# Top-k attention and capacity routing: a longer lag between the steps of a hand-ordered pipeline, and part of a division on VectorE

## The chip, the core and the metric

The kernel runs on one core of a Trainium2 chip. The core has five engines with instruction queues of their own, each working in order: TensorE (PE, with its weight loads shown as PEld), VectorE (DVE), ScalarE (ACT), GpSimd (POOL) and SyncE (SP, which here only issues transfers). They meet through semaphores: an instruction waits until others, on other engines, have finished. SBUF is the on-chip memory of 128 partitions, PSUM the memory that TensorE writes its results into. The metric is the device time of one execution, in microseconds.

## The reference

Attention over 8 batches, 8 heads, 576 positions and 64 dimensions, in which every row of scores keeps only its 32 largest; then a mixture of 8 experts in which each token goes to its best expert and each expert keeps at most 80 tokens.

```python
scores = scale * np.matmul(q, k.transpose(0, 1, 3, 2))
kth = np.partition(scores, -top_k, axis=-1)[..., -top_k:-top_k + 1]
mask = scores >= kth
scores = np.where(mask, scores, -1000000000.0)
scores = scores - np.max(scores, axis=-1, keepdims=True)
attn = np.exp(scores)
attn = attn / (np.sum(attn, axis=-1, keepdims=True) + 1e-09)
attn_out = np.matmul(attn, v)                     # (B, H, S, D)
x = attn_out.transpose(0, 2, 1, 3).reshape(B * S, H * D)
logits = x @ w_gate                               # 4608 tokens, 8 experts
expert_idx = np.argmax(logits, axis=1)            # gate_w: softmax weight of the best
# per expert e: the 80 tokens with the largest gate_w
out[tok_idx] = gate_w[tok_idx, None] * (np.maximum(x[tok_idx] @ w1[e], 0.0) @ w2[e])
```

## The kernel before

**Work.** `n` counts the 32 pairs of heads (8 batches times 4 pairs). Of each pair the 576 queries are cut into five tiles `t`: four of 128 rows, and one, `t = NF = 4`, that holds the last 64 rows of both heads. A unit is one head of one tile: 128 rows by 576 scores. So each `n` has 9 units (two each of the tiles 0 to 3, one of tile 4), and there are 288 units `i` and 160 tiles.

**Steps of one unit**, with the names used later (lines of the kernel before):

- `front` (L226, L233): PE makes the scores of a tile in the PSUM tile `sp`, of which there is one; ACT copies them scaled to SBUF, `s`.
- `parts` (L241): DVE takes the 8 largest of each of six blocks of a row, six MAX8 instructions into `cand`.
- `search`: from these 48, DVE takes three times the 8 largest (L252), knocking them out in between (L260). With the 24th largest as bias, ACT writes `sign`, whether each score is below it, with a count (L257). POOL multiplies scores and signs into `y` (L263, the product); DVE takes the 8 largest of `y`, that is, the next ones below (L265, the maximum), and picks the threshold by the count (L268, the pick, with an accumulator read behind it).
- `below` (L277, L279): the mask of scores under the threshold, on ACT for odd units and on POOL for even units.
- `turn_w` (L315 to L324), once per tile: PE transposes scores into the PSUM tiles `ab` (one buffer) and `cc` (two buffers) and adds the masks, scaled to be very negative; ACT takes the exponential into `wT`, first of `cc`, then of `ab`.
- `back` (L335): PE multiplies `wT` with v, into the free half of the same `cc`. v has a column of ones, so that the sums of the weights come out as well.
- `over` (L347): DVE takes the reciprocal of these sums, into `z_all`.
- `divide` (L358): the result times the reciprocal goes to `xn`, as two ACT instructions per tile.
- `norm` (L367 to L394), once per `n` in four pieces over later steps: SP stores `xn`; PE turns it (L201), ACT copies it (L375), PE multiplies it with the gate (L380), ACT copies the result (L387), and for three of four `n` DVE adds it to the logits (L391). Every second batch `gates` follows (L402 to L425), a dozen small DVE instructions.

**Order.** The order on each engine is the order in which `run` records it: it is written by hand, and no scheduler moves anything. `step(i)` records one step; the letters of a string say what comes when on DVE, with POOL and ACT instructions recorded where they fall:

```python
back = dict(a=0, b=1, c=1, d=1, e=1, y=2, g=3, h=4, m=4, H=3, M=3)
for c in "GybGcGdGeGGzag" if i % 2 else "GGbghHmMyGcGdGeGza":
```

`G` is one MAX8 of unit `i`; `a` to `e` are the three rounds and two knock-outs, `e` with the sign on ACT; `y` is the product, `g` the maximum, `h` and `H` the pick, `m` and `M` the mask, `z` the reciprocal. The number is the lag: `y=2` records in step `i` the product of unit `i - 2`. Even steps hold the masks and picks of two units, odd steps none. After the letters a step records `turn_w` for the tile whose last unit is `i - 4`, then `divide`, the `front` of unit `i + 4`, `back` for the tile of `i - 5`, at times the turn of the next q and k (`turn`, L201 and L214), and pieces of `norm`. Behind a half tile (`rest`), `back` of the tile before it comes first.

**Buffers.** `s` has 5 buffers (a tile each), `sign`, `y`, `wT` and `xn` 2, `mask` 3, `cand` 3, the other small tiles 4, v (`vb`) 3. q, k and v of `n + 2` are loaded by SP in the step of the unit (t = 2, h = 1) of `n`; in others SP also sends one transfer of expert weights or one that clears part of the output (`slow`).

After the loop come `route` (choosing tokens, mostly DVE) and the experts (mostly PE); neither is touched.

Of the kernel before, what the change touches and what calls it, by code (L numbers as in the profile page):

```python
# [27 lines left out]
def kernel(  # L28
# [11 lines left out]
    nc = tc.nc  # L40
# [108 lines left out]
    class Attention:  # L149


        def __init__(self, stack, lean):
            self.lean = lean
            pool = lambda name, bufs, **kw: stack.enter_context(tc.tile_pool(name=name, bufs=bufs, **kw))
            self.nat, self.qkp, self.rows = pool("nat", 1), pool("qkp", 2), pool("rows", 2)
            self.small, vpool = pool("small", 4), pool("vpool", 1)
            self.ps_s, self.ps_w, self.ps_c = (pool(n, k, space=PSUM) for n, k in (("ps_s", 1), ("ps_w", 1), ("ps_c", 2)))
            self.qk, self.turned, self.lg = {}, {}, {}
            self.s, self.top, self.cnt, self.y, self.mask, self.w, self.xn = ({} for _ in range(7))
            self.thr, self.z = thr_all, z_all  # L160
            self.odd = set()


            self.vb = []
            for j in range(1 if lean else 3):
                t = vpool.tile([P, NK, 2, D + 1], F32, name=f"vb{j}")
                nc.gpsimd.memset(t[:, :, :, D : D + 1], 1.0)
                nc.gpsimd.memset(t[: P - TL, NF, :, :], 0.0)
                self.vb.append(t)

            self.xT = vpool.tile([P, NK * P], F32, name="xT")
            nc.gpsimd.memset(self.xT[:, S:], 0.0)

        def load(self, n, b, hp):
            one = bass.ds(b, 1)
            tiles = []
            for name, src in (("qn", q), ("kn", k)):
                t = self.nat.tile([P, NK, 2, D], F32, name=name, tag=name)
                for h in range(2):
                    nc.sync.dma_start(  # L180
                        t[:, 0:NF, h, :],
                        src[one, 2 * hp + h, : NF * P, :].rearrange("o (c p) d -> p (o c) d", p=P))
                nc.sync.dma_start(
                    t[0:TL, NF, :, :], src[one, 2 * hp : 2 * hp + 2, NF * P :, :].rearrange("o h p d -> p (o h) d"))
                tiles.append(t)
            t = self.vb[n % len(self.vb)]
            for h in range(2):
                nc.sync.dma_start(
                    t[:, :NF, h, :D], v[one, 2 * hp + h, : NF * P, :].rearrange("o (c p) d -> p (o c) d", p=P))
            nc.sync.dma_start(  # L190
                t[P - TL :, NF, :, :D], v[one, 2 * hp : 2 * hp + 2, NF * P :, :].rearrange("o h p d -> p (o h) d"))
            self.qk[n] = tiles

        def four(self):
            return self.ps_s.tile([P, 4, 512], F32, name="sp", tag="sp")
# [20 lines left out]
        def front(self, n, t):  # L216

            qT, kT = self.turned[n]
            m = P if t < NF else TL
            i = n * UPP + 2 * t  # L220
            ps = self.four()
            for j in range(2):
                for h in range(2):
                    d = slice(D * h, D * h + D)
                    o = ps[:, 2 * h + j, :HS] if t < NF else ps[TL * h : TL * h + TL, j, :HS]
                    nc.tensor.matmul(o, lhsT=qT[d, t * P : t * P + m], rhs=kT[d, j * HS : (j + 1) * HS], start=True, stop=True)  # L226
            g = 2 if t < NF else 1
            s = self.rows.tile([P, 2 * S], F32, name="s", tag="s", bufs=2 if self.lean else 5)
            for h in range(g):
                self.s[i + h] = s[:, h * S : (h + 1) * S]  # L230
            for j in range(0, 2 * g, 2 if i == 0 else 2 * g):
                w = 2 if i == 0 else 2 * g
                nc.scalar.activation(s[:, j * HS : (j + w) * HS].rearrange("p (j c) -> p j c", c=HS), ps[:, j : j + w, :HS],  # L233
                                     Act.Copy, scale=TINY)
# [10 lines left out]
        def search(self, i):  # L245

            s, cand = self.s[i], self.top[i]
            top = self.top[i] = self.small.tile([P, G0 // 8 - 1, 8], F32, name="top", tag="top")
            w9 = self.small.tile([P, 16], F32, name="w9", tag="w9")
            for r in range(G0 // 8):  # L250
                dst = top[:, r, :] if r < G0 // 8 - 1 else w9[:, :8]
                nc.vector.max(out=dst, in_=cand)  # L252
                if r == G0 // 8 - 1:

                    sign = self.rows.tile([P, S], BF16, name="sign", tag="sign")
                    cnt = self.small.tile([P, 1], F32, name="cnt", tag="cnt")
                    nc.scalar.activation(sign, s, Act.Sign, bias=w9[:, 7:8], scale=-1.0, accum_out=cnt)  # L257
                yield
                if r < G0 // 8 - 1:
                    nc.vector.match_replace(out=cand, in_to_replace=dst, in_values=cand, imm_value=LOW)  # L260
                    yield
            y = self.rows.tile([P, S], F32, name="y", tag="y")
            nc.gpsimd.tensor_tensor(out=y, in0=s, in1=sign, op=Alu.mult)  # L263
            yield
            nc.vector.max(out=w9[:, 8:], in_=y)  # L265
            yield
            pick = self.small.tile([P, TOP_K - G0 + 1], F32, name="pick", tag="pick")
            nc.vector.scalar_tensor_tensor(out=pick, in0=past, scalar=cnt, in1=w9[:, 7:], accum_out=self.thr[:, i : i + 1],  # L268
                                           op0=Alu.is_equal, op1=Alu.mult)
            yield  # L270

        def below(self, i):

            self.top.pop(i)
            self.mask[i] = self.rows.tile([P, S], BF16, name="mask", tag="mask", bufs=3)
            if i in self.odd:
                nc.scalar.activation(self.mask[i], self.s[i], Act.Relu, bias=self.thr[:, i : i + 1], scale=-1.0)  # L277
                return
            nc.gpsimd.tensor_scalar(self.mask[i], self.s[i], self.thr[:, i : i + 1], None, op0=Alu.is_lt)  # L279
# [69 lines left out]
        def divide(self, n, t):  # L349
            if t == 0:  # L350
                self.xn[n] = self.rows.tile([P, NK, 2, D], F32, name="xn", tag="xn")
            cc = self.w.pop((n, t))
            for h in range(2):
                if t < NF:
                    p, o, j, m = slice(0, P), 2 * P + h * (D + 1), h, P
# [71 lines left out]
        def run(self, slow):  # L427

            units = []
            for n in range(NP):  # L430
                for t in range(NF):
                    units += [(n, t, 0), (n, t, 1)]
                units.append((n, NF, 2))
            self.odd = set(range(1, NU, 2))
            first, second = {}, {}
            later = []
            due = []
            drawn = []
            ready = {}

            def whole(i):
# [3 lines left out]
            def step(i, last):  # L445
                if 0 <= i < NU:
                    n, t, h = units[i]
                    if t == 2 and h == 1 and n + 2 < NP:
                        self.load(n + 2, *divmod(n + 2, HP))
                    if t in (1, 3) and h == 0 and slow and n:  # L450
                        slow.pop(0)()
                    if t == 0 and h == 0 and n + 1 < NP:
# [1 line left out]
                    first[i] = self.parts(i)  # L454


                back = dict(a=0, b=1, c=1, d=1, e=1, y=2, g=3, h=4, m=4, H=3, M=3)
                for c in "GybGcGdGeGGzag" if i % 2 else "GGbghHmMyGcGdGeGza":
                    if c == "G":
                        if 0 <= i < NU:  # L460
                            next(first[i])
# [3 lines left out]
                            second[i] = self.search(i)  # L465
                            next(second[i])
                    elif c == "z":
                        for u in drawn:
                            self.over(*u)
                    elif c in "mM":  # L470
                        if 0 <= i - back[c] < NU:
                            self.below(i - back[c])
                    elif i - back[c] in second:
                        next(second[i - back[c]])
                done = list(drawn)
                drawn.clear()

                def back():
                    if whole(i - 5):
                        self.back(*units[i - 5][:2])  # L480
                        drawn.append(units[i - 5][:2])


                rest = whole(i - 4) and units[i - 4][2] == 2
                if rest:
                    back()
                if whole(i - 4):
                    self.turn_w(*units[i - 4][:2])
                for u in done:
                    self.divide(*u)  # L490

                ends = [(n, range(NK) if n < NP - 1 else range(NF) if t < NF else range(NF, NK))
                        for n, t in done if t == NF or (n == NP - 1 and t == NF - 1)]
# [20 lines left out]
                    ready[later[-1]] = 0  # L514

            with tc.manual_schedule():
                self.load(0, 0, 0)
                self.load(1, *divmod(1, HP))
                nc.sync.dma_start(wg, moe_w_gate.rearrange("(c p) e -> p c e", p=P))
                self.turn(0)  # L520
                i = -4
                while i < NU + 6 or later:
                    step(i, i >= NU + 5)
                    i += 1
            assert not slow and not due

        def batch(self, b):

            for hp in range(HP):
                self.load(hp, b, hp)  # L530
                self.turn(hp)
                for t in range(NK):
                    self.front(hp, t)
# [381 lines left out]
```

## Time and profile before

| | |
|---|---|
| median of 3 runs | 994.47 us (993.04 to 995.51) |
| profiled execution: its own time | 994.13 us |
| its span, first to last instruction | 992.4 us |
| mean granted TensorE clock | 0.983 |
| attention loop | until about 868 us |
| POOL product L263 | 288, mean 1280 ns |
| POOL mask L279 | 144, mean 1722 ns |
| DVE maximum L265 | 288, mean 752 ns |
| ACT division L358 | 320, 86.6 us busy |

The span is what the profile shows of the execution. Busy time is the time in which an engine had an instruction running. Idle time before an instruction is put down to whoever released it last. Instructions on DVE and ACT overlap a little at their ends, so that the distance from start to start is shorter than a duration.

### The profile page before, as it was taken

To read this page: it belongs to the slowest core of one execution; us is meant where nothing else is said; L and a number is where in the kernel's file an instruction comes from. 1 tells how busy PE (TensorE), PEld (TensorE's weight loads), DVE (VectorE), ACT (ScalarE), POOL (GpSimd) and SP (SyncE) were. 2 spreads that over 40 slices of the span, in tenths; PEclk is the share of its full clock that TensorE was granted. 3 is DMA by queue.
4 is the path that set the end of the run, shared out by engine and by line. 5 is a ranking of instruction groups with operands and counts; after the bars stand their busy time and mean duration, and the time that the engine had idled before them with its cause. 6 is when DMAs were issued, how large, how long until landed. Compare 5 with 4: busy or idle time off the path is not lost.

```text
span 992.4 us, 35679 instructions
## 1 busy us (share of the span) xinstructions
PE 881.3 (89%) x13368; PEld 710.3 (72%) x13368; DVE 804.6 (81%) x4928; ACT 798.2 (80%) x1652; POOL 627.3 (63%) x474
## 2 busy tenths in 40 slices
PE   5899999999989999999899999999899998689996
PEld 3677777777767777777677777777677776578896
DVE  5798989898989898999989898989898989471110
ACT  3899999999989999999899999999899999501110
POOL 3677767676767777777677676766677777402111
PEclk9999999999999999999999999999999999979999
DMA  3445453333323233333111122222222200084921
GB/s 72 102 123 133 126 135 91 92 92 92 93 76 77 75 87 86 88 90 92 46 41 44 44 50 50 51 50 49 49 50 50 50 13 14 16 339 147 368 85 29
DMA packets 167797, 85.76 MB, mean 86 GB/s; under 512 B 117696, under 2 KB 154560, under 8 KB 167616
## 3 DMA queue, kind: packets, MB, share of 16 engines
q1 hardware_dynamic: 166592, 80.78, 29.1%
q0 software_dynamic: 1024, 2.62, 0.9%
q8 instruction: 107, 1.75, 0.7%
q14 instruction: 74, 0.61, 0.2%
HBM read 63.19 MB, written 20.19 MB: 84 GB/s over the span
## 4 chain that ended last, share of the span: by engine, by line
DVE 46%; PE 26%; ACT 15%; POOL 7%; issue 5%; DMA 1%; POOLq 0%; SPq 0%; DVEq 0%; ACTq 0%
DVE cand L241 15%; DVE w L265 11%; DVE cand L260 6%; PE cc L335 5%; DVE top L252 5%; ACT sign L257 5%; POOL y L263 5%; PE sp L226 4%; PE yp L799 4%; DVE pick L268 3%; ACT wT L324 3%; ACT mask L277 3%; PE sp L201 2%; DVE w L252 2%; POOL mask L279 2%
## 5 line engine op out<-in xcount | busy, mean ns | idle before, releaser
L241 DVE MAX8 cand<-s 128x8 f32<-128x96 f32 x1728 | 400.6, 246 | 9.0 <-ACT s L233 8.8
L263 POOL TENSOR_TENSOR y<-s,sign 128x576 f32<-128x576 f32 x288 | 365.3, 1280 | 65.9 <-ACT sign L257 65.9
L279 POOL TENSOR_SCALAR mask<-s,thr_all 128x576 bf16<-128x576 f32 x144 | 247.9, 1722 | 178.3 <-DVE pick L268 175.4
L335 PEld LDWEIGHTS cc<-vb,wT 128*64 128x64 f32 x5760 | 182.8, 139 | 113.6 <-ACT wT L324 100.1
L265 DVE MAX8 w<-y 128x8 f32<-128x576 f32 x288 | 216.4, 752 | 45.8 <-POOL y L263 45.8
L335 PE MATMUL cc<-vb,wT 128*64 128x65 f32 x5760 | 205.2, 226 | 42.7 <-ACT wT L324 42.7
L257 ACT ACTIVATE sign<-s,w 128x576 bf16<-128x576 f32 x288 | 225.2, 782 | 7.1 <-POOL y L263 3.0
L226 PE MATMUL sp<-both 64*128 64x288 f32 (+1 forms) x1280 | 203.2, 437 | 17.5 <-ACT part L387 9.5
L233 ACT ACTIVATE s<-sp 128x1152 f32<-128x1152 f32 (+1 forms) x161 | 167.4, 1040 | 12.2 <-PE sp L226 9.9
L315 PE MATMUL ab<-ident,s 128*128 128x128 f32 x1148 | 176.2, 283 | 0.0
L324 ACT ACTIVATE wT<-ab 128x1024 f32<-128x1024 f32 (+1 forms) x159 | 149.1, 937 | 0.0
L226 PEld LDWEIGHTS sp<-both 64*128 64x128 f32 (+1 forms) x1280 | 106.1, 180 | 56.4 <-ACT part L387 11.4
L315 PEld LDWEIGHTS ab<-ident,s 128*128 128x128 f32 x1148 | 127.9, 142 | 11.6 <-issue 0.9
L252 DVE MAX8 top<-cand 128x8 f32<-128x48 f32 x576 | 116.0, 201 | 4.5
L277 ACT ACTIVATE mask<-s,thr_all 128x576 bf16<-128x576 f32 x144 | 112.4, 781 | 6.9 <-DVE pick L268 6.5
L320 PEld LDWEIGHTS <-mask 128*128 128x128 bf16 x1440 | 94.2, 98 | 31.9 <-POOL mask L279 29.2
L260 DVE MATCH_REPLACE8 cand<-top,cand 128x48 f32<-128x48 f32 x576 | 110.9, 193 | 0.0
L358 ACT ACTIVATE xn<-cc,z_all 128x64 f32<-128x64 f32 (+1 forms) x320 | 86.6, 320 | 1.2 <-DVE z_all L347 0.8
L315 PE MATMUL cc<-ident,s 128*128 128x128 f32 x288 | 79.1, 275 | 0.0
L322 ACT ACTIVATE wT<-cc 128x256 f32<-128x256 f32 (+1 forms) x160 | 56.9, 356 | 16.8 <-PE cc L320 15.5
L268 DVE SCALAR_TENSOR_TENSOR pick<-past,cnt,w 128x9 f32<-128x9 f32 x288 | 60.3, 223 | 0.3 <-ACT xn L358 0.3
L257 ACT ACTIVATION_READ_ACCUMULATOR sign<-s,w 128x1 f32 x288 | 58.7, 204 | 0.0
(187 smaller groups left out, 909.4 us busy)
## 6 DMA issues: line engine op xcount, KB each, us to landing
w<-in_moe_w_dram SPq DMA_DIRECT2D x10, 2048.0 KB, 11.6
w<-in_moe_w_dram SPq DMA_DIRECT2D x24, 512.0 KB, 4.6
out_dram<-zero SPq DMA_DIRECT2D x9, 1024.0 KB, 6.5
qn<-in_q_dram SPq DMA_DIRECT2D x64, 128.0 KB, 2.5
kn<-in_k_dram SPq DMA_DIRECT2D x64, 128.0 KB, 2.5
vb<-in_v_dram SPq DMA_DIRECT2D x64, 128.0 KB, 2.7
xd<-xn SPq DMA_DIRECT2D x32, 256.0 KB, 3.8
qn<-in_q_dram SPq DMA_DIRECT2D x32, 32.0 KB, 2.3
```

The costliest lines, as they stand in the source:

```text
L226: nc.tensor.matmul(o, lhsT=qT[d, t * P : t * P + m], rhs=kT[d, j * HS : (j + 1) * HS], start=True, stop=True)
L233: nc.scalar.activation(s[:, j * HS : (j + w) * HS].rearrange("p (j c) -> p j c", c=HS), ps[:, j : j + w, :HS], Act.Copy, scale=TINY)
L241: nc.vector.max(out=cand[:, j, :], in_=s[:, j * S // NG : (j + 1) * S // NG])
L252: nc.vector.max(out=dst, in_=cand)
L257: nc.scalar.activation(sign, s, Act.Sign, bias=w9[:, 7:8], scale=-1.0, accum_out=cnt)
L260: nc.vector.match_replace(out=cand, in_to_replace=dst, in_values=cand, imm_value=LOW)
L263: nc.gpsimd.tensor_tensor(out=y, in0=s, in1=sign, op=Alu.mult)
L265: nc.vector.max(out=w9[:, 8:], in_=y)
L279: nc.gpsimd.tensor_scalar(self.mask[i], self.s[i], self.thr[:, i : i + 1], None, op0=Alu.is_lt)
L315: nc.tensor.matmul(dst[h][c], lhsT=sc[:, keys[c]], rhs=ident, start=c == 0 or (c == NF and h == 0), stop=False, is_transpose=True, skip_gr ...
L324: nc.scalar.activation(wT[:, : g * NF, :], ab.rearrange("p h c r -> p (h c) r")[:, : g * NF, :], Act.Exp, scale=scale / TINY)
L335: nc.tensor.matmul(cc[r : r + TL, o], lhsT=wT[:, h * NF + c if c < NF else 2 * NF + h, r : r + TL], rhs=vb[:, c, h if t < NF else r // TL, ...
```

## The change

- The lags grow: `y` 2 to 3, `g` 3 to 4, `h` and `m` 4 to 5, `H` and `M` 3 to 4; `turn_w` is recorded for unit `i - 6` (`LT`) and `back` for `i - 7`. Between `back` and the reciprocal lie two steps instead of one (`drawn`, three lists).
- A new letter `x` records `divide` two or three DVE instructions behind `z`, ahead of `turn_w`, where it stood behind `turn_w`. `z` moves forward in the string.
- For the tiles `t` = 0 and 1 the division is one DVE instruction, a product of the sums in PSUM with the reciprocals, over both heads. The others stay on ACT.
- Buffers: `s` 5 to 7, `sign` 2 to 3, `mask` 3 to 4, the small tiles 4 to 7.
- v's load is a function of its own, recorded two units later than q's and k's.

In the kernel after, the product is L266, the maximum L268, the pick L271, POOL's mask L282, `turn_w` L318 to L327, `back` L338, the reciprocal L350, the new DVE division L359, ACT's L367, the logit add L400.

```diff
--- before.py
+++ after.py
@@ -153,7 +153,7 @@
             self.lean = lean
             pool = lambda name, bufs, **kw: stack.enter_context(tc.tile_pool(name=name, bufs=bufs, **kw))
             self.nat, self.qkp, self.rows = pool("nat", 1), pool("qkp", 2), pool("rows", 2)
-            self.small, vpool = pool("small", 4), pool("vpool", 1)
+            self.small, vpool = pool("small", 7), pool("vpool", 1)
             self.ps_s, self.ps_w, self.ps_c = (pool(n, k, space=PSUM) for n, k in (("ps_s", 1), ("ps_w", 1), ("ps_c", 2)))
             self.qk, self.turned, self.lg = {}, {}, {}
             self.s, self.top, self.cnt, self.y, self.mask, self.w, self.xn = ({} for _ in range(7))
@@ -183,13 +183,16 @@
                 nc.sync.dma_start(
                     t[0:TL, NF, :, :], src[one, 2 * hp : 2 * hp + 2, NF * P :, :].rearrange("o h p d -> p (o h) d"))
                 tiles.append(t)
+            self.qk[n] = tiles
+
+        def load_v(self, n, b, hp):
+            one = bass.ds(b, 1)
             t = self.vb[n % len(self.vb)]
             for h in range(2):
                 nc.sync.dma_start(
                     t[:, :NF, h, :D], v[one, 2 * hp + h, : NF * P, :].rearrange("o (c p) d -> p (o c) d", p=P))
             nc.sync.dma_start(
                 t[P - TL :, NF, :, :D], v[one, 2 * hp : 2 * hp + 2, NF * P :, :].rearrange("o h p d -> p (o h) d"))
-            self.qk[n] = tiles
 
         def four(self):
             return self.ps_s.tile([P, 4, 512], F32, name="sp", tag="sp")
@@ -225,7 +228,7 @@
                     o = ps[:, 2 * h + j, :HS] if t < NF else ps[TL * h : TL * h + TL, j, :HS]
                     nc.tensor.matmul(o, lhsT=qT[d, t * P : t * P + m], rhs=kT[d, j * HS : (j + 1) * HS], start=True, stop=True)
             g = 2 if t < NF else 1
-            s = self.rows.tile([P, 2 * S], F32, name="s", tag="s", bufs=2 if self.lean else 5)
+            s = self.rows.tile([P, 2 * S], F32, name="s", tag="s", bufs=2 if self.lean else 7)
             for h in range(g):
                 self.s[i + h] = s[:, h * S : (h + 1) * S]
             for j in range(0, 2 * g, 2 if i == 0 else 2 * g):
@@ -252,7 +255,7 @@
                 nc.vector.max(out=dst, in_=cand)
                 if r == G0 // 8 - 1:
 
-                    sign = self.rows.tile([P, S], BF16, name="sign", tag="sign")
+                    sign = self.rows.tile([P, S], BF16, name="sign", tag="sign", bufs=3)
                     cnt = self.small.tile([P, 1], F32, name="cnt", tag="cnt")
                     nc.scalar.activation(sign, s, Act.Sign, bias=w9[:, 7:8], scale=-1.0, accum_out=cnt)
                 yield
@@ -272,7 +275,7 @@
         def below(self, i):
 
             self.top.pop(i)
-            self.mask[i] = self.rows.tile([P, S], BF16, name="mask", tag="mask", bufs=3)
+            self.mask[i] = self.rows.tile([P, S], BF16, name="mask", tag="mask", bufs=4)
             if i in self.odd:
                 nc.scalar.activation(self.mask[i], self.s[i], Act.Relu, bias=self.thr[:, i : i + 1], scale=-1.0)
                 return
@@ -350,6 +353,12 @@
             if t == 0:
                 self.xn[n] = self.rows.tile([P, NK, 2, D], F32, name="xn", tag="xn")
             cc = self.w.pop((n, t))
+            if t < 2:
+
+                sums = cc[:, 2 * P : 2 * P + 2 * (D + 1)].rearrange("p (h d) -> p h d", h=2)[:, :, :D]
+                nc.vector.tensor_tensor(out=self.xn[n][:, t, :, :], in0=sums, op=Alu.mult,
+                                        in1=self.z[:, n % NP, t, :].unsqueeze(2).to_broadcast([P, 2, D]))
+                return
             for h in range(2):
                 if t < NF:
                     p, o, j, m = slice(0, P), 2 * P + h * (D + 1), h, P
@@ -432,10 +441,11 @@
                     units += [(n, t, 0), (n, t, 1)]
                 units.append((n, NF, 2))
             self.odd = set(range(1, NU, 2))
+            LT = 6
             first, second = {}, {}
             later = []
             due = []
-            drawn = []
+            drawn = [[], [], []]
             ready = {}
 
             def whole(i):
@@ -447,6 +457,8 @@
                     n, t, h = units[i]
                     if t == 2 and h == 1 and n + 2 < NP:
                         self.load(n + 2, *divmod(n + 2, HP))
+                    if t == 3 and h == 1 and n + 2 < NP:
+                        self.load_v(n + 2, *divmod(n + 2, HP))
                     if t in (1, 3) and h == 0 and slow and n:
                         slow.pop(0)()
                     if t == 0 and h == 0 and n + 1 < NP:
@@ -454,8 +466,8 @@
                     first[i] = self.parts(i)
 
 
-                back = dict(a=0, b=1, c=1, d=1, e=1, y=2, g=3, h=4, m=4, H=3, M=3)
-                for c in "GybGcGdGeGGzag" if i % 2 else "GGbghHmMyGcGdGeGza":
+                back = dict(a=0, b=1, c=1, d=1, e=1, y=3, g=4, h=5, m=5, H=4, M=4)
+                for c in "GybGczGdxGeGGag" if i % 2 else "GGbghHmMyGcGdzGexGa":
                     if c == "G":
                         if 0 <= i < NU:
                             next(first[i])
@@ -465,29 +477,30 @@
                             second[i] = self.search(i)
                             next(second[i])
                     elif c == "z":
-                        for u in drawn:
+                        for u in drawn[0]:
                             self.over(*u)
+                    elif c == "x":
+                        for n, t in drawn[0]:
+                            self.divide(n, t)
                     elif c in "mM":
                         if 0 <= i - back[c] < NU:
                             self.below(i - back[c])
                     elif i - back[c] in second:
                         next(second[i - back[c]])
-                done = list(drawn)
-                drawn.clear()
+                done = drawn.pop(0)
+                drawn.append([])
 
                 def back():
-                    if whole(i - 5):
-                        self.back(*units[i - 5][:2])
-                        drawn.append(units[i - 5][:2])
-
-
-                rest = whole(i - 4) and units[i - 4][2] == 2
+                    if whole(i - LT - 1):
+                        self.back(*units[i - LT - 1][:2])
+                        drawn[1].append(units[i - LT - 1][:2])
+
+
+                rest = whole(i - LT) and units[i - LT][2] == 2
                 if rest:
                     back()
-                if whole(i - 4):
-                    self.turn_w(*units[i - 4][:2])
-                for u in done:
-                    self.divide(*u)
+                if whole(i - LT):
+                    self.turn_w(*units[i - LT][:2])
 
                 ends = [(n, range(NK) if n < NP - 1 else range(NF) if t < NF else range(NF, NK))
                         for n, t in done if t == NF or (n == NP - 1 and t == NF - 1)]
@@ -514,13 +527,14 @@
                     ready[later[-1]] = 0
 
             with tc.manual_schedule():
-                self.load(0, 0, 0)
-                self.load(1, *divmod(1, HP))
+                for n in range(2):
+                    self.load(n, *divmod(n, HP))
+                    self.load_v(n, *divmod(n, HP))
                 nc.sync.dma_start(wg, moe_w_gate.rearrange("(c p) e -> p c e", p=P))
                 self.turn(0)
                 i = -4
-                while i < NU + 6 or later:
-                    step(i, i >= NU + 5)
+                while i < NU + LT + 3 or later:
+                    step(i, i >= NU + LT + 2)
                     i += 1
             assert not slow and not due
 
@@ -528,6 +542,7 @@
 
             for hp in range(HP):
                 self.load(hp, b, hp)
+                self.load_v(hp, b, hp)
                 self.turn(hp)
                 for t in range(NK):
                     self.front(hp, t)
```

## The prediction

> **What bounds the kernel now.** I read the page first, then stretches of the span, then one repeating window.
>
> ```profile
> PE 881.3 (89%) x13368; PEld 710.3 (72%) x13368; DVE 804.6 (81%) x4928; ACT 798.2 (80%) x1652; POOL 627.3 (63%) x474
> ...
> DVE 46%; PE 26%; ACT 15%; POOL 7%; issue 5%; DMA 1%; POOLq 0%; SPq 0%; DVEq 0%; ACTq 0%
> ```
>
> The shares alone name no bound: the last 125 us are another stage (routing and experts), which the change leaves alone. In the attention stage, which ends at about 868 us, the timeline repeats. The masks on POOL start at 391.01 and, nine masks (18 units, 10 tiles) later, at 442.72; earlier and later windows also last 51.71 to 51.72, and those that hold a `gates` block 54 to 55.4. The steady part, 43 to 855 us, holds 138 masks, so about 15 such windows. The busy times of one, and its waits:
>
> ```profile
> 391.01:442.72 51.71, 47.43 (x696) 37.62 (x692) 47.63 (x302) 48.87 (x102) 38.05 (x28) 1.00 0.33 89
> ```
> ```profile
> POOL mask L279 <- DVE pick L268: 11.6, 10, 1.7
> PEld cc L335 <- ACT wT L324: 6.1, 8, 1.3
> POOL y L263 <- ACT sign L257: 3.1, 4, 1.2
> DVE w L265 <- POOL y L263: 2.5, 3, 1.2
> ...
> ACT both L214 <- PE sp L201: 1.3, 2, 1.0
> DVE z_all L347 <- PE cc L335: 1.3, 1, 1.3
> ```
>
> PE (47.43), DVE (47.63) and ACT (48.87) are each 92 to 95% busy at full clock: nothing is far from being the bound, and what costs time is waiting on one another. DVE waits 3.78 in the window: 2.5 for POOL's product (0.69, 0.64 and 1.16 in the timeline) and 1.29 for PE before one reciprocal. Five of the nine mask-to-mask distances are 5.31 long, and the four longer ones hold these waits. Here is one of them:
>
> ```profile
> 401.26 1.28 POOL L263 TENSOR_TENSOR y<-s,sign 128x576 f32<-128x576 f32 x1 [0.72 <-ACT sign L257]
> 403.64 1.72 POOL L279 TENSOR_SCALAR mask<-s,thr_all 128x576 bf16<-128x576 f32 x1 [1.10 <-DVE pick L268]
> ...
> 402.57 0.76 DVE L265 MAX8 w<-y 128x8 f32<-128x576 f32 x1 [0.69 <-POOL y L263]
> ```
>
> The sign on ACT was late (behind another sign and a mask), so POOL started its product 0.72 late and DVE stood 0.69 for it. The second line is a loop: POOL product, DVE maximum, DVE pick, POOL mask. Every mask waits at least 1.10 on it.
>
> A 5.31 distance is full on both sides: DVE runs 403.59 to 408.90 without a wait, and POOL needs 1.69 (mask, start to start) + 2.52 (two products) + 1.10 = 5.31. So the floors of a window are 51.71 − 3.78 = 47.93 for DVE and 9 × 5.31 = 47.8 for the POOL loop.
>
> **The change, part by part, per window.**
>
> *Lag between sign and product, and between sums and reciprocal.* A product now comes a whole step (about 2.87) later than its sign, against delays of 0.6 to 1.2 now. The reciprocal comes two steps after the sums, against a wait of 1.29. I take all 3.78 off. What is late next: the loop through POOL and the PE–ACT exchange, both below.
>
> *Multiply on VectorE.* Tiles t = 0 and 1: four multiplies per window, 64 in all, each reading 128 sums from PSUM and the reciprocals from SBUF. No such instruction is in the trace. The nearest rows:
>
> ```profile
> L347 DVE RECIPROCAL z_all<-cc 128x2 f32<-128x2 f32 x128 | 19.5, 152 | 5.7 <-PE cc L335 5.6
> L810 DVE TENSOR_SCALAR y<-yx,a 80x512 f32<-80x512 f32 x8 | 6.0, 746 | 40.1 <-PE yx L808 40.1
> L412 DVE TENSOR_TENSOR oh<-oh,mx 128x80 f32<-128x80 f32 x4 | 4.1, 1028 | 0.1
> L773 DVE COPY xt<-xp 128x320 f32<-128x320 f32 x8 | 3.9, 492 | 38.7 <-PE xp L771 38.7
> ```
>
> From the two PSUM readers, (746 − 492)/192 = 1.32 ns an element, so 492 − 192 × 1.32 = 239 ns for 128; rows on DVE overlap by some 20 to 80 ns, so 0.22 us. The low end is 0.10 (the 40-element add, start to next start), the high end 1.29: the 80-element L412 starting at 268.92 beside a product ran until that product ended. I take 0.22, since PSUM rows (the reciprocal too, never over 0.17) show no such hold: 4 × 0.22 = +0.88.
>
> The Trainium skill, page "SBUF — State Buffer", section "Who interferes with whom", says that a VectorE instruction with two SBUF inputs is held by a GpSimd instruction that reads SBUF, and one with a single SBUF input is not. By that rule the new multiply, whose sums lie in PSUM, keeps 0.22; the same rule speaks against the change at the logit add, next. The trace agrees only in part: the add at 421.47 took 0.18 beside POOL's mask, which reads SBUF.
>
> *Logit adds.* In the new order 14 adds (8 before) stand right after an odd step's maximum. There POOL was idle waiting for a sign; now it will be inside the second product, of which 1.26 − 0.66 = 0.6 remains. L412 shows such an add held to the product's end. 14 × 0.6 = 8 us, +0.55 per window.
>
> *ACT relieved.* 128 activations of L358 at 67.1/256 = 0.262 go: 33.5 us, 8 × 0.262 = 2.10 per window, so ACT falls from 48.87 to 46.77. ACT was the fullest engine but stood on no wait of DVE by itself, so this buys no time directly; it pays for the PE–ACT exchange.
>
> *The POOL loop is not loosened.* This decides the size. POOL masks even units, and the even unit's product is now issued in an odd step and its maximum, pick and mask all in the next even step. POOL's order stays mask, product, product, and the mask still waits for the maximum of the product just before it. Worse, the mask now needs the second of two picks instead of the first: pick to pick is 0.18 and the second's accumulator read ends 0.03 later in its own run, so 1.10 becomes about 1.28 and the loop 5.49 (ends: 5.31 if latency hides it, 5.52). Nine of them: 49.4. On DVE the four distances with a multiply have 5.33 + 0.22 = 5.55. Taking the larger each time, 4 × 5.55 + 5 × 5.49 = 49.65, plus the adds 0.55: 50.2.
>
> *PE and ACT.* PE has 47.43 of work and still meets exponentials late where a copy, mask and sign stand between (0.85 at 441.49). With ACT at 46.77 I let 0.1 come back: 50.3. The ends are 0 and, if all PE's waits stay, 51.5.
>
> *Accumulator tile `cc`.* It is held a step longer with two buffers. At each move from t = 3 over the half tile to the next pair, PE's next transposes into `cc` stand in the same step as that tile's division. PE then runs 2 to 3 us behind DVE. That is covered: signs have the added step, scores are made four steps ahead, sums have two. If the cover is gone, see the slower rival.
>
> *One answer, nothing: more buffers, and v's load moved.* On SP's queue v's three transfers pass one weight or clearing transfer and come two steps later; they land in 2.7 us and are read about 18 steps (50 us) later. The weight transfer that moves ahead of v no longer stands behind v's wait for PE.
>
> *Ends.* At the start distances of 8.15 and 7.68 include POOL waiting 2.2 to 2.9 for signs; I give −1. The drain gains one more pair on PE (turn 1.85, sums 1.32) and one product (1.26), beside PE waits of 1.17, 0.57 and 1.23 after 852 us; I give +1.
>
> **Sum.** 15 × (51.71 − 50.3) = 21. The profiled execution took 994.13 with a span of 992.4, 0.3 below the median of 994.47. 994.13 − 21 − 1 + 1 = 973. A difference under 0.3%, 3 us, can't be told from none.
>
> **Rivals.**
>
> *All waits go (0.17).* The second pick costs the loop nothing and adds are not held: DVE alone bounds, 47.93 + 0.88 = 48.8 to 49.3, gain 2.4 to 2.9 per window, 36 to 43 us: about 955. For: five distances are wait-free on DVE now. Against: POOL must then hand over in 1.10 or less.
>
> *The waits only change name (0.14).* PE's 4.1 us of waits on ACT and on POOL per window stay, 47.43 + 4.1 = 51.5: gain 0.2 × 15, about 991. For: PE waited 0.2 to 0.85 on exponentials in most pairs. Against: at 398.01 PE passes without waiting when ACT is ready, and ACT loses 2.1.
>
> *Slower by `cc` (0.09).* Two such moves per window. PE has 51.71 − 47.43 = 4.28 spare, 2.14 for each move; if each costs PE a full step, 2.87, the window grows by 2 × (2.87 − 2.14) = 1.5, or 22 us: about 1016. It decides from 2.14 us of PE wait per move. Against: the wait can only be as long as PE is early.
>
> *Slower by held multiplies (0.05).* At L412's 1.29 each, 47.93 + 5.2 + 0.55 = 53.6, +1.9 per window: about 1022. It breaks even at (3.78 − 0.55)/4 = 0.81 per multiply. Against: it reads one SBUF tensor, and half of them stand beside a mask.
>
> *It doesn't do what it says.* As shown, the added step is real for sign and product but not for the even unit's product to mask; this is in the forecast.
>
> **How the numbers follow.** The forecast has 0.55, own range 966 to 981 (loop 5.40 to 5.52, PE return 0 to 0.4). Faster: 0.55 + 0.17 + 0.06 of the third case = 0.78; within 0.3%: 0.08 of it; slower: 0.14. The range 955 to 993 leaves out the slower cases and some below.
>
> **What would show it.** Right: DVE's maxima wait under 0.5 per window for late signs, POOL's sign waits vanish, the mask's wait on picks is 1.25 to 1.35 each time, reciprocals never wait, the multiply's mean is 0.22 to 0.30, adds behind the maximum take about 0.6, the window is about 50.3. Wrong: POOL queues without waiting for picks, a window of 51 or more with PE waiting for `cc` on a division, or multiplies near 1.3.

## The result, and the profile after

The kernel after takes 1046.68 us (median of 4 runs, 1046.23 to 1052.31) against 994.48 for the kernel before on the same chip: ratio 1.0539, interval 1.0501 to 1.0577. The forecast of 973 us was wrong in sign.

In the profiled executions the span grew by 52.8 us (1045.2 against 992.4). The last block maximum of the attention loop starts 47.0 us later (894.08 against 847.07), the way from there to PE's first instruction of the routing is 7.2 longer (28.9 against 21.7), and the rest 1.4 shorter. So it is the loop, and a little its drain. One of its windows after, nine mask distances from 576.92 to 632.11, now 55.19 long, in the windows view (length; busy time of PE, PEld, DVE, ACT and POOL, with their instructions; granted clock, DMA share, GB/s) and in the waits (us in total, times, longest):

```profile
576.92:632.11 55.19, 47.73 (x695) 37.58 (x692) 49.59 (x306) 47.78 (x96) 37.97 (x27) 1.00 0.19 45
```
```profile
POOL mask L282 <- PE cc L323: 7.4, 3, 4.1
...
PE cc L318 <- ACT xn L367: 3.8, 4, 1.5
ACT wT L325 <- PE cc L323: 3.5, 5, 1.4
POOL mask L282 <- PE sp L229: 3.3, 2, 2.0
DVE w L268 <- POOL y L266: 3.0, 2, 2.7
PE cc L338 <- ACT wT L327: 2.4, 4, 1.0
DVE z_all L350 <- PE cc L338: 1.8, 2, 1.1
```

PE, ACT and POOL have hardly more work than before, or less: 47.73, 47.78 and 37.97, against 47.43, 48.87 and 38.05. DVE has 1.96 more, 49.59 against 47.63: 1.1 are the four multiplies, 0.6 the logit adds. The fourth experiment below takes the multiplies out and gets slower, so they are not the loss. The rest are waits, with new names among them. POOL's waits for signs in this window go from 3.1 to 0.8; it waits for PE instead. PE waits before its transposes into `cc` for ACT's division. DVE still waits 4.8 a window (3.0 and 1.8), more than the 3.78 of before. Over the whole span, before:

```profile
POOL y L263 <- ACT sign L257: 65.9, 63, 12.0
DVE w L265 <- POOL y L263: 45.8, 49, 2.8
...
DVE z_all L347 <- PE cc L335: 27.3, 18, 4.5
```

and after, where PE's wait for the division is a line that the kernel before doesn't have:

```profile
POOL mask L282 <- PE cc L323: 88.6, 39, 4.1
...
PE cc L318 <- ACT xn L367: 58.8, 61, 2.5
```

Eight of the nine distances are 5.51 to 6.51; the largest, 8.28, is where the pair after a half tile begins. Here it is in another window (799.47 to 854.67, 55.20 long), in the timelines of PE, ACT and POOL, and with a wait of DVE from the same window's beginning (start, duration, engine, instruction, wait):

```profile
813.01 0.33 PE L318 MATMUL cc<-ident,s 128*128 128x128 f32 x1 [0.58 <-ACT xn L367]
```
```profile
811.60 0.76 ACT L260 ACTIVATE sign<-s,w 128x576 bf16<-128x576 f32 x1
...
812.43 0.53 ACT L367 ACTIVATE xn<-cc,z_all 128x64 f32<-128x64 f32 x2
...
814.32 0.38 ACT L325 ACTIVATE wT<-cc 128x256 f32<-128x256 f32 x1 [0.60 <-PE cc L323]
```
```profile
814.27 1.72 POOL L282 TENSOR_SCALAR mask<-s,thr_all 128x576 bf16<-128x576 f32 x1 [4.08 <-PE cc L323]
```
```profile
802.32 0.17 DVE L350 RECIPROCAL z_all<-cc 128x2 f32<-128x2 f32 x1 [1.12 <-PE cc L338]
```

The division of the tile two before stands behind a sign in ACT's queue. PE's transposes into `cc` wait for it, the exponential waits for PE, and POOL's mask waits 4.08 for a mask buffer that this late turn has to empty. Behind that mask stand two products, and DVE's maxima wait for those (the next one 2.70, at 817.27). The following tile's turn waits again, 1.14 at 818.78, for the half tile's division.

### The profile page after: what moved, and what is told of

Its sections match the earlier page's. It is cut to its first block, busy times and chain, and to the rows that moved or that the text cites. A ratio compares the mean times of both kernels' runs of the same rounds, so it can differ in the third digit from the quotient of the medians.

```text
span 1045.2 us, 35876 instructions
## 1 busy us (share of the span) xinstructions
PE 891.3 (85%) x13368; PEld 713.2 (68%) x13368; DVE 833.9 (80%) x4992; ACT 777.7 (74%) x1524; POOL 626.1 (60%) x474
## 3 DMA queue, kind: packets, MB, share of 16 engines
q1 hardware_dynamic: 166592, 80.78, 27.3%
## 4 chain that ended last, share of the span: by engine, by line
PE 43%; ACT 26%; DVE 15%; issue 12%; POOL 3%; DMA 1%; ACTq 0%; POOLq 0%; SPq 0%; DVEq 0%
PE sp L229 9%; ACT sign L260 8%; PE cc L338 8%; ACT mask L280 7%; PE sp L204 6%; ACT wT L327 4%; DVE cand L244 4%; PE ab L318 4%; PE yp L814 4%; ACT xn L367 3%; DVE w L268 3%; PE ab L323 3%; PE cc L318 3%; POOL y L266 2%; DVE cand L263 2%
## 5 line engine op out<-in xcount | busy, mean ns | idle before, releaser
L282 POOL TENSOR_SCALAR mask<-s,thr_all 128x576 bf16<-128x576 f32 x144 | 247.9, 1721 | 265.1 <-PE cc L323 88.6
L266 POOL TENSOR_TENSOR y<-s,sign 128x576 f32<-128x576 f32 x288 | 364.2, 1282 | 29.6 <-ACT sign L260 28.6
L338 PEld LDWEIGHTS cc<-vb,wT 128*64 128x64 f32 x5760 | 182.7, 139 | 118.0 <-ACT wT L327 102.7
L268 DVE MAX8 w<-y 128x8 f32<-128x576 f32 x288 | 217.5, 755 | 41.3 <-POOL y L266 39.2
L338 PE MATMUL cc<-vb,wT 128*64 128x65 f32 x5760 | 205.0, 226 | 46.4 <-ACT wT L327 44.3
L260 ACT ACTIVATE sign<-s,w 128x576 bf16<-128x576 f32 x288 | 222.2, 772 | 2.2 <-DVE w L255 1.4
L229 PE MATMUL sp<-both 64*128 64x288 f32 (+1 forms) x1280 | 208.0, 446 | 6.4 <-ACT s L236 4.5
L318 PE MATMUL ab<-ident,s 128*128 128x128 f32 x1148 | 179.4, 283 | 0.0
L327 ACT ACTIVATE wT<-ab 128x1024 f32<-128x1024 f32 (+1 forms) x159 | 148.6, 935 | 0.0
L229 PEld LDWEIGHTS sp<-both 64*128 64x128 f32 (+1 forms) x1280 | 108.7, 184 | 47.8 <-ACT s L236 7.9
L318 PEld LDWEIGHTS ab<-ident,s 128*128 128x128 f32 x1148 | 128.7, 142 | 10.2 <-issue 0.8
L318 PE MATMUL cc<-ident,s 128*128 128x128 f32 x288 | 83.2, 289 | 60.9 <-ACT xn L367 58.8
L323 PEld LDWEIGHTS <-mask 128*128 128x128 bf16 x1440 | 97.4, 100 | 2.0
L318 PEld LDWEIGHTS cc<-ident,s 128*128 128x128 f32 x288 | 40.8, 142 | 75.8 <-ACT xn L367 75.6
L271 DVE SCALAR_TENSOR_TENSOR pick<-past,cnt,w 128x9 f32<-128x9 f32 x288 | 59.2, 220 | 0.7 <-ACT sign L260 0.3
L350 DVE RECIPROCAL z_all<-cc 128x2 f32<-128x2 f32 (+1 forms) x160 | 25.7, 161 | 42.5 <-PE cc L338 39.6
```

The costliest lines, as they stand in the source:

```text
L318: nc.tensor.matmul(dst[h][c], lhsT=sc[:, keys[c]], rhs=ident, start=c == 0 or (c == NF and h == 0), stop=False, is_transpose=True, skip_gr ...
L327: nc.scalar.activation(wT[:, : g * NF, :], ab.rearrange("p h c r -> p (h c) r")[:, : g * NF, :], Act.Exp, scale=scale / TINY)
L338: nc.tensor.matmul(cc[r : r + TL, o], lhsT=wT[:, h * NF + c if c < NF else 2 * NF + h, r : r + TL], rhs=vb[:, c, h if t < NF else r // TL, ...
```

## The experiments

Ratios are to the kernel before on the same chip, with their intervals.

**Masks or accumulator (1 to 4).**

```diff
-  self.mask[i] = ...(name="mask", tag="mask", bufs=4)      # 1 and 3
+  self.mask[i] = ...(name="mask", tag="mask", bufs=8)
-  drawn[1].append(units[i - LT - 1][:2])                   # 2 and 3: reciprocal one step after the sums
+  drawn[0].append(units[i - LT - 1][:2])
-  if t < 2:                                                # 4: ACT divides all tiles
+  if False:
```

> The kernel after with 8 buffers for the masks instead of 4, nothing else. Theory A (mask buffers): POOL's mask of an even step reuses a buffer that PE frees in a turn recorded only one or two steps before, so PE's lateness holds POOL, and POOL holds DVE; then the 181 us in which POOL waits for PE or for ACT's exponentials before a mask go, the 8.28 distances fall to about 5.5, and the time is 975 to 990. Theory B (cc): PE waits for the divisions that empty the accumulator tile, which is held one step longer; then the PE waits for ACT's division (58.8 us) stay and the time stays above 1025. Theory C (ring): the two waits are one ring and either cure opens it: 980 to 1000, with PE's waits for the division smaller as well.

1045.79 us, ratio 1.0529 (1.0501 to 1.0556). The waits view of the whole span:

```profile
POOL y L266 <- ACT sign L260: 69.7, 44, 12.7
DVE z_all L350 <- PE cc L338: 66.5, 43, 4.3
...
PE cc L318 <- ACT xn L367: 60.0, 62, 2.5
```

POOL's 88.6 us of waiting for PE's turn are down to 3.0, and the time is the same. The sign waits are up from 28.6 to 69.7 and the reciprocals' from 39.6 to 66.5. The mask buffers only carried PE's lateness to POOL; without them signs and sums carry it. PE's wait for the division is what did not move. Theories A and C fall.

> The kernel after with reciprocal and division one step after the sums, as before the change, so that cc is emptied one step sooner; masks keep 4 buffers. Theory A: the masks still wait for PE, time above 1025. Theory B: PE's waits for the division go and the time is 975 to 990. Theory C: 980 to 1000, POOL's waits for PE small as well.

1010.44 us, ratio 1.0162 (1.0136 to 1.0188): 36 us back. PE's wait for the division goes from 58.8 to 7.6, POOL's wait for PE's turn from 88.6 to 2.8:

```profile
PE cc L318 <- ACT xn L367: 7.6, 16, 0.5
```

The edit also starts `norm` a step sooner, which follows the division. Theory B, but only for some two thirds of the loss; the time lies outside all three stated ranges.

> Both: 8 mask buffers, and reciprocal and division one step after the sums. Theories A, B and C: what remains is the loop product, maximum, two picks, mask at 5.5 a pair, 965 to 980. If something else carries the loss, above 1000.

1009.11 us, ratio 1.0151 (1.0131 to 1.0171): more mask buffers add nothing, and something else carries a further 15 us. Reciprocals still wait 51.1 us for PE, and PE 76.4 for exponentials:

```profile
PE cc L338 <- ACT wT L327: 76.4, 130, 3.8
DVE z_all L350 <- PE cc L338: 51.1, 47, 4.2
```

> The kernel after with all five tiles divided by ACT, nothing else. Theories A, B and C: the multiply on DVE costs little (64 at about 0.25 us) and ACT's 33 us more make PE's waits for ACT a little longer: 1040 to 1065. Theory D (the multiply on DVE is the loss, by holding DVE beside POOL): below 1000.

1058.08 us, ratio 1.0645 (1.0625 to 1.0665). The multiply on DVE is no part of the loss; it brings 11 us. Theory D falls.

**What else stands in the new order (5 to 9).** All strings are the even and odd steps' letters.

```diff
   # early reciprocal: "GybGczGdxGeGGag" if i % 2 else "GGbghHmMyGcGdzGexGa"
+  # 5: picks swapped:  odd the same;  even "GGbgHhMmyGcGdzGexGa"
+  # 6 and 9: late z:   "GybGcGdGeGGzaxg";  even "GGbghHmMyGcGdGeGzax"
+  # 7: both:           "GybGcGdGeGGzaxg";  even "GGbgHhMmyGcGdGeGzax"
   # 5, 6, 7 with drawn[0].append, 9 with drawn[1].append as in the kernel after
   # 8: the kernel before, with the `if t < 2` branch of the kernel after in divide
```

> The early reciprocal (1010 us), and the two picks of an even step in the other order, so that POOL's mask waits for the first of them. If the second pick carries what is left of the loss, the usual mask distance falls from 5.46 to 5.51 to about 5.31 and the time to 985 to 992. If the reciprocal's waits for PE carry it, the time stays within 1003 to 1012.

1021.97 us, ratio 1.0277 (1.0254 to 1.0301): slower than without the swap. POOL's waits before a mask stay at 1.24 to 1.43. The pick now uses the maximum just before it:

```profile
424.28 0.76 DVE L268 MAX8 w<-y 128x8 f32<-128x576 f32 x1
425.08 0.23 DVE L271 SCALAR_TENSOR_TENSOR pick<-past,cnt,w 128x9 f32<-128x9 f32 x1
```

It starts 0.04 after that maximum's end, where in the order of before it started 0.08 ahead of the end of a maximum it doesn't read (403.25 against 403.33). So the swap gives 0.14, in some steps 0.19, the distance of the two picks in the second experiment, and takes 0.12, in some steps 0.19. That it costs 11.5 us goes with the odd unit's pick, which now comes second: ACT waits 10.2 us for picks before its masks instead of 2.0, and PE 85.9 for exponentials instead of 76.6. No run separates this.

> The early reciprocal (1010 us), with reciprocal and division at the place in the step that the reciprocal had before the change, about 1.5 us later in DVE's order. If the reciprocal's waits for PE (51 us in all, 2.8 a window) carry the loss, they fall below 25 us and the time is 980 to 992. If PE is late for another reason, the waits only move, 1003 to 1012.

994.91 us, ratio 1.0006 (0.9993 to 1.0018): another 15.5 us back, level with the kernel before. Reciprocals wait 34.5 instead of 51.4. The change had moved `z` forward by six letters in odd steps and three in even ones; asked for one step after the sums, an early `z` comes before PE is done.

> Both at once: picks swapped, reciprocal and division late in the step. If the two causes are separate and add up: 960 to 978, below the kernel before. If one of them only hides the other: 985 to 995.

996.39 us, ratio 1.0021 (0.9999 to 1.0042): the swap adds nothing here.

> The kernel before with the tiles 0 and 1 divided by DVE, at the place where the division stood; lags, buffers and strings as before. If ACT's load made the late signs, 975 to 988. If DVE's 64 multiplies (0.22 each, 14 us) cost what ACT saves, 988 to 998. If the multiply at this place waits for PE and ACT, above 1000.

989.74 us, ratio 0.9946 (0.9933 to 0.996). The multiply alone makes the kernel before a little faster; sign waits fall from 65.9 to 56.5 and product waits from 45.8 to 32.6.

> The kernel after (two steps between sums and reciprocal) with reciprocal and division late in the step, as in the sixth experiment. It holds cc about half a step longer than the kernel after, and asks for the sums half a step later. If the holding of cc is what costs, it is slower than 1046.7: 1055 to 1085, with PE waiting longer for the division. If the early place of the reciprocal in DVE's order is what costs, it is faster: 990 to 1030.

1067.42 us, ratio 1.0738 (1.072 to 1.0756). The late place, which brought 15.5 us at one step, costs 21 at two. What differs in the waits is PE's for the division, since `cc` is held half a step longer:

```profile
POOL mask L282 <- PE cc L323: 116.7, 40, 6.0
...
PE cc L318 <- ACT xn L367: 72.7, 62, 2.5
DVE w L268 <- POOL y L266: 69.8, 67, 4.8
```

PE's wait for the division rises from 58.8 to 72.7, while the reciprocals' own wait falls from 39.6 to 28.8. The two edits pull against each other: a later reciprocal waits less and frees `cc` later. With two buffers only one step between sums and reciprocal has room for it.

**What is left: the lags and the division's place (10 to 15).** 10 to 12 start from the sixth experiment.

```diff
-  if t < 2:                                        # 10: ACT divides all tiles
+  if False:
-  self.odd = set(range(1, NU, 2))                  # 11 and 12: masks exchanged
+  self.odd = set(range(0, NU, 2))
-  ... else "GGbghHmMyGcGdGeGzax":                  # 12: odd unit's pick and mask ahead of the maximum
+  ... else "GGbhmgHMyGcGdGeGzax":
```

> The sixth experiment (994.9 us: late reciprocal one step after the sums) with ACT dividing all tiles: what is left of the change is the longer lag of product, pick, mask and turn, and the buffers. If the longer lag of the sign is worth the 3.1 us a window that POOL waited for signs: 980 to 993. If the second pick and the later turn take that back: 998 to 1012.

1020.26 us, ratio 1.0254 (1.0234 to 1.0274): the multiply was hiding 25 us here. ACT and PE show why, in their timelines:

```profile
502.94 0.50 ACT L367 ACTIVATE xn<-cc,z_all 128x64 f32<-128x64 f32 x2
503.34 0.38 ACT L325 ACTIVATE wT<-cc 128x256 f32<-128x256 f32 x1
503.60 1.03 ACT L327 ACTIVATE wT<-ab 128x1024 f32<-128x1024 f32 x1
```
```profile
504.69 0.51 PE L338 MATMUL cc<-vb,wT 128*64 128x65 f32 x10 [1.42 <-ACT wT L327]
```

Recorded with the letters, the division stands ahead of the exponentials, and PE's sums wait for it. In the order of before it stands behind them (433.25, 433.51, then 434.42).

> The sixth experiment with the masks exchanged: POOL masks odd units, ACT even ones, so that POOL waits for the first of the two picks. If the second pick costs 0.2 a pair, POOL's wait before a mask goes from 1.25 to 1.31 down to 1.10 and the time to 975 to 987. If DVE's own work is the bound, nothing changes: 992 to 998.

1000.58 us, ratio 1.0057 (1.0037 to 1.0077). The shortest distances do fall, from 5.46 to 5.52 down to 5.31 to 5.43, and the time doesn't: around a half tile the distances are up to 7.03 and 6.62, and the reciprocals wait 54.7 us for PE instead of 34.5. The second pick's 0.2 was real and not the bound.

> The same with the odd unit's pick and POOL's mask ahead of the next maximum, so that the loop product, maximum, pick, mask no longer closes on the product just finished. If that loop is what bounds the sixth experiment, POOL's wait before a mask falls to about 0.5 and the time to 960 to 980. If DVE, PE and ACT bound it, 985 to 998.

996.04 us, ratio 1.0019 (1.0005 to 1.0034). The loop through POOL is open, products no longer hold DVE (0.4 us over the whole span), and nothing is gained. POOL's wait before a mask stays at 1.09 to 1.37 mostly, where 0.5 was expected, and most of it is still for DVE's picks (153.9 us).

```diff
-  for c in "GybGcGdGeGGzaxg" if i % 2 else "GGbghHmMyGcGdGeGzax":    # 13, from the sixth
+  for c in "GybGcGdGeGGzag" if i % 2 else "GGbghHmMyGcGdGeGza":
       if whole(i - LT):
           self.turn_w(*units[i - LT][:2])
+      for u in done:
+          self.divide(*u)
   # 14: 13 with ACT dividing all tiles; 15: the same edit on the twelfth
   # 16: the eighth with `if t < 3`; 17: 13 with LT = 5; 18: 13 with `if t < 3`
```

> The sixth experiment (994.9 us) with the division recorded behind the turn, as before the change, so that in ACT's queue it stands behind the exponentials: left of the change are the lags of product, pick, mask and turn, the buffers and the multiply. If the division ahead of the exponentials makes PE wait for them, PE's wait for the exponentials falls from 60 to below 45 us and the time is 970 to 986. If the lags themselves cost, 992 to 1000.

986.86 us, ratio 0.9931 (0.9914 to 0.9947): the fastest of all, faster than both kernels. PE's wait for exponentials falls, though not below the 45 expected, and the time is 8 us less. The sixth experiment, then this one:

```profile
PE cc L338 <- ACT wT L327: 60.4, 114, 3.3
```
```profile
PE cc L338 <- ACT wT L327: 54.3, 83, 2.6
```

The edit also moves the odd steps' multiplies on DVE behind the maximum; the next experiment, against the tenth, has no multiplies.

> The same with ACT dividing all tiles: the lags and buffers alone, against the kernel before. If the division's place was the loss of the tenth experiment (1020 us), 980 to 996. If the lags lose, above 1005.

995.5 us, ratio 1.0015 (1.0002 to 1.0028). The lags and buffers alone, with everything else as before, bring nothing. The waits of the whole span:

```profile
DVE z_all L350 <- PE cc L338: 47.8, 62, 4.1
...
POOL y L266 <- ACT sign L260: 13.9, 2, 12.7
...
DVE w L268 <- POOL y L266: 7.8, 6, 3.1
```

The longer lag does what it says: products wait for signs 13.9 (before 65.9), maxima for products 7.8 (before 45.8). But reciprocals wait 47.8 (before 27.3), and the usual distances are 5.46 to 5.88 instead of 5.31. Against the tenth, the division's place alone is worth 25 us with ACT dividing everything, and PE's wait for exponentials goes from 84.2 to 55.1.

> The twelfth experiment (996 us: masks exchanged, pick and POOL's mask ahead of the next maximum) with the division behind the turn. If PE's waits for the exponentials were what bounded it: 960 to 980. If DVE bounds it: 985 to 996.

987.4 us, ratio 0.9927 (0.9911 to 0.9944): level with the thirteenth. The loop through POOL bounds neither.

> The eighth experiment (989.7 us: kernel before, tiles 0 and 1 divided by DVE) with tile 2 divided by DVE as well. If each multiply relieves ACT by more than it costs DVE: 984 to 989. If DVE is the bound by now: 990 to 996.

990.66 us, ratio 0.9962 (0.9947 to 0.9977): a third tile on DVE adds nothing to the eighth.

> The thirteenth experiment (986.9 us) with the turn at lag 5 instead of 6, so that PE's sums come one step sooner after the masks. If the reciprocal's waits that remain (34 us) come from PE working late behind its own queue, they stay and the time is 984 to 990. If the later turn itself makes the sums late, the waits fall below 20 us: 970 to 982. If the turn now waits for masks of its own step, above 992.

1040.68 us, ratio 1.0459 (1.044 to 1.0478). At lag 5 the turn no longer falls in the step that records a `front` (unit `i + 4` is then a second head), and PE's scores wait for ACT instead, 45.2 us for the turned output's copy alone:

```profile
DVE z_all L350 <- PE cc L338: 100.6, 81, 3.4
...
PE sp L229 <- ACT xT L384: 45.2, 30, 1.8
...
PE cc L338 <- ACT wT L327: 21.1, 36, 1.2
```

So it doesn't answer its question. PE waits less for exponentials than in the thirteenth (21.1 against 54.3) and much more to write scores (109.6 in all, for three copies on ACT that read `sp`): the edit changes which steps hold both a turn and a `front`, and the time is 54 us longer.

> The thirteenth experiment with tile 2 divided by DVE as well. If ACT's work still bounds through PE's waits for exponentials: 980 to 985. If DVE's floor bounds: 987 to 992.

990.57 us, ratio 0.9963 (0.9948 to 0.9977): 4 us worse than with two tiles, in the range that was given for a bound by DVE's own work. The 32 further multiplies, of 0.273 each, add 8.7 us to DVE's work; that they are the reason isn't shown otherwise.

**The sum, from before to after.** Lags and buffers alone: +1 (14). Multiply on DVE: −9 (13 against 14). Division ahead of the exponentials: +8 (6 against 13). Reciprocal early in the step: +15.5 (2 against 6). Second step between sums and reciprocal: +36 (after against 2). Together 52, each taken in this order; the ninth experiment shows that the last two don't add in another. Some of these runs are from different chips, on which the kernel before takes 993.73 to 994.89, so the +1 is not told from nothing.

## Why the prediction was wrong

**The failed step is "Accumulator tile `cc`", costed at nothing.** The prediction said that PE running behind is covered by the sign's added step, early scores and two steps for sums. It isn't: PE waited 58.8 us for divisions, and this came back to DVE by whichever way was open: mask buffers in the kernel after, signs and sums in the first experiment. One step less of holding, the one line of the second experiment, took 58.8 down to 7.6 and 36 us off the time. The slower rival "by `cc`" (0.09, about 1016) named the place. It counted two such moves a window and PE's 4.28 us as spare, with no loss up to 2.14 of PE wait per move. The profile shows two waits at each move, 3.8 us a window or 1.9 per move, and the window grew by 3.48 all the same: the spare was not PE's to spend, since PE needs it for its waits on ACT's exponentials (2.4 a window still).

**The places of the reciprocal and the division were not costed.** `z` moved forward was worth 15.5 us at one step; `x` ahead of the exponentials 8, and 25 without the multiply. Both are plain in the strings. The prediction's own row, PE waiting 0.85 at 441.49 because a copy, mask and sign stood ahead of the exponential, was the price tag for putting one more instruction there.

**"I take all 3.78 off" failed.** Product waits do go with the lag (13.9 and 7.8 in the fourteenth experiment), but in the kernel after DVE waits 4.8 a window. The window came out 4.9 above the forecast's 50.3 (55.19), and this is nearly all of it. Even without the loss at `cc`, the lags brought no time by themselves: in the fourteenth experiment (995.5 us) reciprocals wait for PE instead, 47.8 against 27.3.

**ACT's relief "buys no time directly" was mis-sized.** The multiply gave 5 us in the kernel before, 9 with the lags, 11 in the kernel after, 25 with the division ahead of the exponentials. Whether ACT's lesser work gives this, or that these tiles' division no longer stands in ACT's queue, isn't separated.

**The drain was mis-sized.** The prediction gave it +1; the way from the last block maximum to the routing grew by 7.2.

**Right.** The multiply took 0.277 us (0.270 to 0.292, estimated 0.239 ahead of overlap) and was never held beside POOL's products, in which 22 of the 64 began, as the Trainium skill's page "SBUF — State Buffer", section "Who interferes with whom", has it for one SBUF input. The logit adds went from a mean of 0.199 to 0.416 (the 23 of 40 elements): 14 began inside a product, as forecast, and 13 of them took 0.58. The forecast's 8 us for them counted the whole 0.6 and not the increase over 0.18; measured it is 5. The loop through POOL went from 5.31 to 5.51 or 5.52 (forecast 5.49, end 5.52) since the mask waits for the second pick. But it didn't set the time: the eleventh, twelfth and fifteenth experiments shorten or open it without gain.

**Open.** In the best version reciprocals still wait 34.3 us for PE; in the window from 383.86 these are 2.5 us, of which 1.05 fall on the half tile's reciprocal and 1.16 on the next pair's. What would cure that was not found. A third `cc` buffer was not tried.

## What to carry to other kernels

In an in-order pipeline a longer lag between two steps also holds every buffer between them longer; before lengthening one, list which buffers are freed by the later step and who is queued behind their reuse, and lengthen only the lags whose buffers can grow. An instruction that moves in a hand-written order is priced at the place it moves to: here the same division cost 8 to 25 us more ahead of the exponentials that another engine awaited than behind them. And where three engines are 92 to 95% busy, a wait that is removed may only have come last: POOL's 88.6 us of waiting for PE went to 3.0 with more mask buffers, and the time stayed, 1046.68 and 1045.79.

## What the runs showed of the hardware

A DVE instruction that reads what the one just before it wrote starts later. In the fifth experiment the first pick of an even step reads its maximum and began 0.04 us after that maximum's end (425.08), in 97 of 144 cases, and 0.10 to 0.11 in the other 47; in the kernel before it doesn't read it, and began 0.08 ahead of the end (403.25) in all 144.

An add with two SBUF inputs was held by a POOL product with two SBUF inputs: in the kernel after all 14 adds that began inside a product ended 0.06 after it, 13 of them 0.58 long, where the undisturbed ones take 0.18. Beside a POOL mask, which reads one tensor, 15 adds of the kernel before ran at 0.18, at 421.47 for instance. Which difference between product and mask decides isn't shown.
